# A chunked recurrence followed by two networks: chunk products stored from the ScalarE queue, the decays of y loaded in one transfer, y of both halves scaled and stored in one piece

## Chip, cores and metric

The kernel runs on one core of one Trainium2 chip, in one launch. The metric is the device time of an execution in microseconds. TensorE (PE in the profile, its weight loads PEld), VectorE (DVE), ScalarE (ACT) and GpSimd (POOL) each run their own instructions in order; SyncE (SP) only issues transfers. ACT and POOL can issue transfers too. An instruction that waits holds up everything behind it on its engine.

## What is computed

For each of 32 heads (4 batches of 8) a 40x40 state is carried through 768 steps. The result y passes a layer norm, a first network with a residual (320 to 1280 to 320), and a second one (320 to 1024, a convolution of three taps along the sequence, a sigmoid gate, back to 320).

```
for t in range(S):                                   # S = 768, per head
    y[t]  = r[t] @ state
    Sa    = state @ a[t]
    state = state * w[t][None, :] - outer(Sa, b[t]) + outer(v[t], k[t])
xn = layer_norm(y) * g_ln
x  = y + relu(xn @ w_ch1) @ w_ch2
h  = relu(x @ w_in);  out = (h * sigmoid(conv3(h, conv_w))) @ w_out
```

## The kernel before

The sequence is cut into 24 chunks of 32 steps; two chunks are a group G (12 groups), four chunks a block Q (6 blocks of 128 tokens). Inside a chunk the steps are solved together by small matrix products, and only the state goes from chunk to chunk. Each head lies in one of two halves of the partitions: rows 0 to 39 or rows 64 to 103, by the constants XR0, VR0 and ZR0.

Preparation of a group (`stage`): w is loaded (ld_w) and its running products p_g are made (`decay1`, `decay2`, on DVE for the first four groups, on POOL afterwards; the tiles blk, bd and pre carry products across partitions by way of memory); k, a, b are loaded and scaled (`prep1`, `prep2`, tiles p_k, p_b, p_a); the scaled k and b are stored as ks, p_g is stored as gs (`store_g`); all are transposed on PE (L323) and evicted by ACT and DVE. `check` sends w through ACT twice (junk) to see whether its values are in bounds.

`inner(n)` multiplies the transposed pieces of chunk n (PE aps, L397), and ACT scales the products into the tile pst (L402). After the second chunk of a group two transfers store half of pst each to memory as pd (L407), issued from SP. DVE masks pst into the operand l (L413, eight instructions a group, both inputs in SBUF).

`solve(Q)` loads the pd of four chunks as sv (L424) and inverts the unit triangular matrices by 30 pairs of multiply and add (svt L431, sv L433): Q = 0 on DVE, the other five on POOL. The result is stored as td (L434) and loaded in parts as tm (`load_tm`, L444, four loads a group).

`chunk(n)` is the recurrence itself: PE reps (L474), ACT copy re; PE zhps with tm (L487), DVE writes r (L492, four a half); PE xps (L505), DVE writes the next r (L516); PE sps, ACT copy s; PE xrps (L544), ACT copy of r; each for the two halves. `load_stacks` loads v and ks of chunk n + 2 into r and l (L226, L229).

`yout(Q, part)`, four parts a Q, transposes y of the Q before (PE yps), scales it on DVE with the decays gtok (ys, L575: one instruction for each half) and stores it as xs (L578: one store for each half). `load_g` loads gtok for a Q by one transfer for each batch (L372). Then the networks run, by batch and half of the sequence (`load`, L885, reads xs into x), while the weights are still being split into a high and a low part by DVE, ACT and POOL.

What sets the order: the kernel gives every piece a due time (`at`), and a scheduler of the framework lays out each engine's instructions from these, from the dependences and from its own estimates of durations. So an edit in one place can change the order on all engines. Each transfer signals one of eight completion semaphores (DMAHW0 to DMAHW7), given out in turn, and waits until the transfer that had the same one before has ended. The tiles pst, sv, gtok and ys have one buffer each, ld_w has three.

Of the kernel before, what the change touches and what calls it, by code (L numbers as in the profile page):

```python
# [7 lines left out]
F32 = mybir.dt.float32  # L8
# [3 lines left out]
ALU = mybir.AluOpType  # L12
# [3 lines left out]
B, H, S, D = 4, 8, 768, 40  # L16
# [1 line left out]
NCH = S // C  # L18
NG = NCH // 2
NQ = NCH // 4  # L20
XR0 = (64, 0)
VR0 = (0, 64)
ZR0 = (32, 96)
SLOT = 168
MO, VO, GO = (0, 96), (32, 96), (0, 136)
W_MIN, W_MAX = 0.4, 2.0
# [22 lines left out]
YB = 1  # L49
# [14 lines left out]
class Recurrence:  # L64
# [71 lines left out]
    def constants(self):  # L136

        nc = self.nc
        V, P, A = nc.vector, nc.gpsimd, nc.scalar
        z = lambda t, *k: A.copy(t, self.zero[0:t.shape[0]].to_broadcast(list(t.shape)))  # L140
        flat = lambda t: t.rearrange("p a b c -> p (a b c)")
        self.at(-18)
        V.memset(self.zero, 0.0)
        for t, x in zip(self.bound, (W_MIN, -W_MAX)):
            V.memset(t, x)
        sh = self.shift.rearrange("p j (i q) -> p j i q", q=4)
        V.memset(self.shift, 0.0)
        for j in range(3):
            V.tensor_copy(sh[:, j, :, j + 1:4], self.ident.rearrange("p (i q) -> p i q", q=4)[:, :, j:j + 1].to_broadcast(
                [128, 32, 3 - j]))  # L150

        V.tensor_reduce(out=self.notbefore, in_=self.ident.rearrange("p (i q) -> p q i", q=4), op=ALU.add,
                        axis=mybir.AxisListType.X)
        for i in range(1, 4):
            V.tensor_tensor(out=self.notbefore[:, i:i + 1], in0=self.notbefore[:, i:i + 1],
                            in1=self.notbefore[:, i - 1:i], op=ALU.add)
        V.tensor_scalar(self.before, self.notbefore, -1.0, 1.0, op0=ALU.mult, op1=ALU.add)
        for t in self.pd_.values():
            V.memset(t[:, :, 40:64], 0.0)
        P.memset(self.mask, 1.0)  # L160
        for q in range(4):
            m = self.mask[32 * q:32 * q + 32, :]
            P.affine_select(out=m, in_=m, pattern=[[1, C]], base=0, channel_multiplier=-1,
                            compare_op=ALU.is_gt, fill=0.0)
        P.memset(self.l1[0], 0.0)
        P.memset(self.kb[96:128], 0.0)
        V.tensor_scalar(self.nmask, self.mask, -1.0, None, op0=ALU.mult)
        self.at(-16.5)
        for i in range(2):
            z(flat(self.rd[i]))  # L170
            z(flat(self.vt[i][96:128]))
        P.memset(self.l1[1], 0.0)
        self.at(-13)
        V.memset(self.zmask, -1.0)
        for q in range(4):
            c = GO[q & 1] - MO[q & 1]
            V.tensor_scalar(self.zmask[32 * q:32 * q + 32, c:c + C], self.mask[32 * q:32 * q + 32], -1.0, None,
                            op0=ALU.mult)
        for t in self.r1[0]:
            V.memset(t, 0.0)  # L180
        P.memset(self.tm[0], 0.0)
        z(self.tm[1].rearrange("p a b -> p (a b)"))
        for p in self.l2:
            P.memset(p[0][96:128], 0.0)
            P.memset(p[1][0:64], 0.0)
            for h in range(2):
                x0 = XR0[h]
                V.tensor_copy(
                    p[h][x0:x0 + D],
                    self.ident[x0:x0 + D, x0:x0 + D].rearrange("p (o d) -> p o d", o=1).to_broadcast([D, 16, D]))  # L190
        P.memset(self.s[96:128], 0.0)
# [15 lines left out]
    def load(self, G, names):  # L207
        t0 = 64 * G
        for n in names:
            src = getattr(self, n)  # L210
            t = self.ld[n, G] = self.tile([128, 2, 8 * D], f"ld_{n}", LW if n == "w" else 1 if n in "rv" else LO, self.lp if n in "rv" else self.ep2 if n == "w" else self.ep)
            for i in range(2):
                if n in "rv":
                    s = src[:, :, t0:t0 + 64, :].rearrange("b (hp two) (c t) e -> two (b hp) c (t e)", two=2, t=8)[i]
                else:
                    b0 = 2 * (1 - i)
                    s = src[b0:b0 + 2, :, t0:t0 + 64, :].rearrange("b h (c t) e -> (b h) c (t e)", t=8)
                (self.nc.gpsimd if G < 2 and n in "rv" and GQ else self.nc.sync).dma_start(out=t[:, i], in_=s)

# [143 lines left out]

    def store_g(self, G):
        for i in range(2):
            b0 = 2 * (1 - i)
            self.nc.sync.dma_start(out=self.gs[G // 2][b0:b0 + 2, :, 64 * (G % 2):64 * (G % 2) + 64, :].rearrange("b h (c t) e -> (b h) c t e", t=8), in_=self.pdt("g", G)[:, 0:8, 64 * i:64 * i + D])

    def load_g(self, Q):
        self.gtok = self.tile([128, B, H, D], "gtok", 1, self.yp)  # L370
        for b in range(B):
            self.nc.sync.dma_start(out=self.gtok[:, b], in_=self.gs[Q][b].rearrange("h t e -> t h e"))  # L372

    def tr_rv(self, G):
        g = G % 2
# [14 lines left out]
    def inner(self, n):  # L390
        nc = self.nc
        l1 = self.l1[(n // 2) % NL1]
        c = n % 2
        ps = self.ps("aps").rearrange("p (k m) -> p k m", k=8)
        for i in range(16):
            x, kk = i & 1, i >> 1
            nc.tensor.matmul(ps[64 * x:64 * x + 64, kk, :], lhsT=self.kb[:, i, c, :],  # L397
                             rhs=l1[:, i, c, :], start=True, stop=True)
        if c == 0:
            self.pst = self.tile([128, 2, 2, 4, 2, C], "pst", 1, self.ep)  # L400
        pst = self.pst[:, :, c]
        self.inner_act = nc.scalar.mul(pst.rearrange("p x k f t -> p x k (f t)"),  # L402
                                       ps.rearrange("p (k x) m -> p x k m", x=2), -1.0).ins
        if c == 1:
            g = (n // 2) % 2
            for y in range(2):
                nc.sync.dma_start(out=self.pd[n // 4][:, 64 * g + 32 * y:64 * g + 32 * y + 32],  # L407
                                  in_=self.pst[64 * y + 32:64 * y + 64].rearrange("s x c k f t -> s (x c k f) t"))
        lv = l1.rearrange("p (k x y) c m -> p x k y c m", x=2, y=2)
        for y in range(2):  # L410
            for half in range(2):
                v0 = VR0[half]
                nc.vector.tensor_tensor(  # L413
                    out=lv[v0:v0 + C, :, :, y, c, 32 * half:32 * half + C],
                    in0=pst[64 * y:64 * y + C, :, :, half],
                    in1=self.nmask[64 * y:64 * y + C].rearrange("p (o q t) -> p o q t", o=1, q=1).to_broadcast(
                        [C, 2, 4, C]), op=ALU.mult)


    def solve(self, Q, eng):  # L420
# [141 lines left out]
    def yout(self, Q, part):  # L562

        nc = self.nc
        t0 = 128 * (Q % 3)
        b01, h0 = part // 2, 4 * (part % 2)
        ps = self.ps("yps")
        for h in range(4):
            nc.tensor.transpose(ps[:, 104 * h:104 * h + 104],
                                self.yt[Q % 2][:, 8 * b01 + h0 + h].rearrange("p c t -> p (c t)"),  # L570
                                self.ident[0:104, 0:104])
        pv = ps[:, 0:416].rearrange("p (h m) -> p h m", h=4)
        for half in range(2):
            ys = self.tile([128, 4, D], f"ys_{half}", YB, self.yp)
            self.last_out = nc.vector.tensor_tensor(  # L575
                out=ys, in0=pv[:, :, XR0[half]:XR0[half] + D], in1=self.gtok[:, 2 * half + b01, h0:h0 + 4],
                op=ALU.mult).ins
            nc.sync.dma_start(out=self.xs[2 * half + b01][Q // 3][t0:t0 + 128, D * h0:D * h0 + 4 * D],  # L578
                              in_=ys.rearrange("p h e -> p (h e)"))


    def at(self, t):
# [133 lines left out]
DM = H * D  # L716
F1, F2 = 1280, 1024
N1, N2 = F1 // 128, F2 // 128
TG = 384
# [97 lines left out]
class Mlp:  # L817
# [64 lines left out]

    def load(self, g):
        x = self.px.tile([128, NT, DM], F32, tag="x", name="x")
        self.nc.sync.dma_start(out=x, in_=self.xs[g // 2][g % 2].rearrange("(n p) e -> p n e", p=128))  # L885
        self.x2[g] = x

    def norm(self, g):
# [248 lines left out]
def sequential(nc, tc, ctx, ins, xs):  # L1137

    p = ctx.enter_context(tc.tile_pool(name="seq", bufs=1))
    n, step = B * H, 8  # L1140
# [11 lines left out]
    for half in range(2):  # L1152
        with tc.For_i(0, TG, step) as t0:
# [11 lines left out]
                tt(tmp, col(v[:, i]), row(k, i), ALU.mult)  # L1165
                tt(st, st, tmp, ALU.add)
            for i in range(B):
                nc.sync.dma_start(out=xs[i][half][bass.ds(t0, step), :].rearrange("t (h e) -> h t e", h=H),
                                  in_=y[H * i:H * i + H])


def run_kernel(tc, r, k, v, w, a, b, g_ln, w1, w2, w3, cw, w4, out):
    nc = tc.nc
    ins = (r, k, v, w, a, b)
    with ExitStack() as ctx:
# [3 lines left out]
        make_identity(nc, ident)  # L1179
        taps = cp.tile([128, 3, N2], F32, name="taps")  # L1180
        excess = cp.tile([128, 2 * NG], F32, name="excess")
        xs = [[dp.tile([TG, DM], F32, name=f"xs_{i}{j}") for j in range(2)] for i in range(B)]
        early = ExitStack()
        ws = Weights(nc)
        ws.open(ctx.enter_context(tc.tile_pool(name="convert", bufs=1)), RAWB, nc.vector if SUBV else nc.gpsimd)
# [52 lines left out]
```

## Time and profile before

| | us |
|---|---|
| three timed executions | 951.85, 951.68, 940.84 (median 951.68) |
| the profiled execution: its own time | 944.43 |
| the profiled execution: its span | 942.7, mean granted TensorE clock 0.941 |
| busy in it: PE, DVE, ACT, POOL | 820.1, 679.3, 513.7, 273.6 |

The span is the time from the first to the last instruction; 1.7 us of the execution lie around it. All rows further down are of this one execution. Time in a row is counted from the start of the span, the number in brackets is the time the engine stood idle before the row's first instruction, with what ended it.

### The profile page before, as it was taken

How to read it: one execution, taken by the hardware profiler on the slowest of the kernel's cores; microseconds unless marked ns; L12 is line 12 of the kernel's file. 1: busy time of each engine (PE TensorE's matmuls, PEld its weight loads, DVE VectorE, ACT ScalarE, POOL GpSimd, SP SyncE). 2: the span in 40 equal slices, each digit the busy share in tenths (PEclk: the TensorE clock that was granted, in tenths of full speed). 3: DMA queues.
4: the chain of work that ended last, by engine and by line, in shares of the span. 5: the costliest groups of instructions: out<-in, count | busy, mean ns of one | idle time of the engine just before them, and what ended most of it. 6: DMA issues, size and time to landing. Idle time of an engine off the chain costs nothing.

```text
span 942.7 us, 24879 instructions
## 1 busy us (share of the span) xinstructions
PE 820.1 (87%) x9959; PEld 721.8 (77%) x9959; DVE 679.3 (72%) x1646; ACT 513.7 (54%) x1166; POOL 273.6 (29%) x498
## 2 busy tenths in 40 slices
PE   0575587797989999979998898999999999999996
PEld 0454465675767777757767877999999999999996
DVE  8879848677667786779888989785649482756356
ACT  6267255854766766545544357564438362746354
POOL 9403268359339448085112222000000000000000
PEclk9867798997999999998999989999999999999999
DMA  5997784684697585683745541101010000000000
GB/s 153 206 235 193 185 170 97 170 186 98 170 166 182 149 164 110 133 158 91 145 109 153 142 114 50 36 1 36 1 36 15 22 15 2 29 1 15 15 15 32
DMA packets 218544, 94.21 MB, mean 100 GB/s; under 512 B 176860, under 2 KB 207924, under 8 KB 218420
## 3 DMA queue, kind: packets, MB, share of 16 engines
q1 hardware_dynamic: 217524, 90.24, 40.8%
q0 software_dynamic: 896, 2.30, 1.1%
q8 instruction: 80, 1.31, 0.6%
q14 instruction: 44, 0.36, 0.1%
HBM read 63.78 MB, written 28.72 MB: 98 GB/s over the span
## 4 chain that ended last, share of the span: by engine, by line
PE 49%; DVE 20%; DMA 8%; ACT 5%; POOL 4%; issue 3%; SPq 2%; DVEq 0%; ACTq 0%; POOLq 0%
PE ups L946 17%; PE acc L956 9%; PE accb L956 8%; DVE r L492 4%; PE xps L505 3%; DVE l L413 3%; PE tps L924 2%; PE tr L323 2%; POOL sv L433 2%; POOL svt L431 1%; PE xrps L544 1%; PE aps L397 1%; DMA x<-xs 1%; DVE r L460 1%; PE reps L474 1%
## 5 line engine op out<-in xcount | busy, mean ns | idle before, releaser
L492 DVE TENSOR_TENSOR r<-zhps,zmask 32x288 f32<-32x288 f32 x192 | 87.2, 454 | 33.7 <-PE zhps L487 28.1
L964 DVE SCALAR_TENSOR_TENSOR rl<-ups,rh 128x384 fp32r<-128x384 f32 x80 | 44.6, 557 | 82.6 <-ACT rh L963 82.4
L963 ACT ACTIVATE rh<-ups 128x384 fp32r<-128x384 f32 x80 | 39.0, 490 | 105.7 <-PE ups L946 105.1
L505 PE MATMUL xps<-r,l 128*40 128x72 f32 x1536 | 82.0, 239 | 13.2 <-DVE r L492 12.3
L505 PEld LDWEIGHTS xps<-r,l 128*40 128x40 f32 x1536 | 62.7, 122 | 32.8 <-DVE r L492 24.9
L433 POOL TENSOR_TENSOR sv<-sv,svt 128x30 f32<-128x30 f32 (+9 forms) x150 | 83.3, 555 | 9.4
L946 PE MATMUL ups<-xh,w1h 128*128 128x384 f32 x240 | 81.2, 339 | 1.7 <-DVE rl L964 1.3
L431 POOL TENSOR_TENSOR svt<-sv 128x30 f32<-128x30 f32 (+9 forms) x150 | 77.9, 520 | 9.2
L946 PE MATMUL ups<-xh,w1l 128*128 128x384 f32 x240 | 80.6, 336 | 0.0
L413 DVE TENSOR_TENSOR l<-pst,nmask 32x256 f32<-32x256 f32 x96 | 58.3, 607 | 24.5 <-ACT pst L402 23.4
L956 PE MATMUL acc<-w2h,rh 128*128 128x320 f32 x240 | 71.6, 310 | 1.7 <-ACT rh L963 1.7
L956 PE MATMUL acc<-w2l,rh 128*128 128x320 f32 x240 | 71.4, 307 | 0.0
L946 PE MATMUL ups<-xh,w3l 128*128 128x384 f32 x192 | 65.1, 341 | 0.3 <-POOL w3l L806 0.3
L134 ACT COPY yt<-xps 40x256 f32<-40x256 f32 x96 | 35.2, 367 | 55.0 <-DVE r L516 50.5
L946 PE MATMUL ups<-xh,w3h 128*128 128x384 f32 x192 | 64.4, 342 | 0.6 <-ACT h L988 0.4
L956 PE MATMUL accb<-w4h,ph 128*128 128x320 f32 x192 | 59.1, 313 | 0.0
L956 PE MATMUL accb<-w4l,ph 128*128 128x320 f32 x192 | 58.7, 309 | 0.0
L956 PE MATMUL acc<-w2h,rl 128*128 128x320 f32 x240 | 49.8, 312 | 6.0 <-DVE rl L964 6.0
L956 PE MATMUL accb<-w4h,pl 128*128 128x320 f32 x192 | 53.4, 311 | 0.6 <-DVE pl L1010 0.6
L946 PE MATMUL ups<-xl,w1h 128*128 128x384 f32 x160 | 53.5, 335 | 0.0
L999 DVE SCALAR_TENSOR_TENSOR c<-h,taps,c 128x256 f32<-128x256 f32 (+1 forms) x88 | 43.9, 508 | 12.8 <-ACT c L997 12.6
L516 DVE TENSOR_TENSOR r<-xps,ge 40x320 f32<-40x320 f32 x96 | 46.7, 486 | 8.3 <-PE xps L505 6.1
(190 smaller groups left out, 2219.4 us busy)
## 6 DMA issues: line engine op xcount, KB each, us to landing
l<-ks SPq DMA_DIRECT2D x44, 160.0 KB, 3.5
raw<-in_moe_w_ch_dram SPq DMA_DIRECT2D x17, 320.0 KB, 3.4
ks<-p_b SPq DMA_DIRECT2D x12, 416.0 KB, 3.3
ks<-p_k SPq DMA_DIRECT2D x12, 416.0 KB, 4.0
ld_w<-in_w_dram SPq DMA_DIRECT2D x24, 160.0 KB, 3.3
ld_k<-in_k_dram SPq DMA_DIRECT2D x24, 160.0 KB, 4.2
ld_a<-in_a_dram SPq DMA_DIRECT2D x24, 160.0 KB, 3.7
ld_b<-in_b_dram SPq DMA_DIRECT2D x24, 160.0 KB, 3.8
```

Source lines behind the costliest of these rows:

```text
L134: return self.nc.scalar.copy(out, in_).ins
L413: nc.vector.tensor_tensor(out=lv[v0:v0 + C, :, :, y, c, 32 * half:32 * half + C], in0=pst[64 * y:64 * y + C, :, :, half], in1=self.nmask[6 ...
L431: eng.tensor_tensor(out=tmp, in0=sv[:, 0:u, u:u + 1].to_broadcast([128, u, m]), in1=sv[:, u:u + 1, u + 1:C].to_broadcast([128, u, m]), op= ...
L433: last = eng.tensor_tensor(out=sv[:, 0:u, u + 1:C], in0=sv[:, 0:u, u + 1:C], in1=tmp, op=ALU.add)
L492: nc.vector.tensor_tensor(out=r1[z0:z0 + 32, :, x, MO[y]:MO[y] + 72], in0=ps[32 * q:32 * q + 32], in1=self.zmask[32 * q:32 * q + 32].rearr ...
L505: nc.tensor.matmul(ps[x0:x0 + D, j >> 2, o:o + 72], lhsT=l2[:, i, :], rhs=r1[:, j, MO[y]:MO[y] + 72], start=True, stop=True)
L516: last = nc.vector.tensor_tensor(out=r2[X0:X0 + D, :, :, VO[y]:VO[y] + D], in0=pv[x0:x0 + D, :, :, v:v + D], in1=ge[X0:X0 + D, :, :, y, c: ...
L946: self.mm = self.nc.tensor.matmul(ps, lhsT=l, rhs=r, start=(i == 0), stop=(i == len(passes) - 1)).ins
L956: self.mm = self.nc.tensor.matmul(acc[n][:, 0:DM], lhsT=l, rhs=r, start=(f == 0 and i == 0), stop=(f == nf - 1 and i == 2)).ins
L963: nc.scalar.activation(rh, ps, AF.Relu)
L964: nc.vector.scalar_tensor_tensor(out=rl, in0=ps, scalar=0.0, in1=rh, op0=ALU.max, op1=ALU.subtract)
L999: nc.vector.scalar_tensor_tensor(out=c, in0=h(1), scalar=w(1), in1=c, op0=ALU.mult, op1=ALU.add)
```

## The change

Three things are edited. The two stores of pst (24 in all) are issued from ACT, in a function of their own. gtok of a Q comes in one load of all four batches (6 in place of 24). y of both halves is scaled by one DVE instruction over 320 elements (24 in place of 48) and stored by one transfer (24 in place of 48); for this xs is one tile for each half of the sequence with all batches in it, and the two halves of the partitions change places (XR0, VR0, ZR0).

```diff
-XR0 = (64, 0)
-VR0 = (0, 64)
-ZR0 = (32, 96)
+XR0 = (0, 64)
+VR0 = (64, 0)
+ZR0 = (96, 32)
...
-        for b in range(B):
-            self.nc.sync.dma_start(out=self.gtok[:, b], in_=self.gs[Q][b].rearrange("h t e -> t h e"))
+        self.nc.sync.dma_start(out=self.gtok.rearrange("t b h e -> t (b h) e"),
+                               in_=self.gs[Q].rearrange("b h t e -> t (b h) e"))
...
         if c == 1:
             g = (n // 2) % 2
-            for y in range(2):
-                nc.sync.dma_start(out=self.pd[n // 4][:, 64 * g + 32 * y:64 * g + 32 * y + 32],
-                                  in_=self.pst[64 * y + 32:64 * y + 64].rearrange("s x c k f t -> s (x c k f) t"))
+            self.pd_store(self.pd[n // 4][:, 64 * g:64 * g + 64])
...
+    def pd_store(self, pd):
+
+        for y in range(2):
+            self.nc.scalar.dma_start(out=pd[:, 32 * y:32 * y + 32],
+                                     in_=self.pst[64 * y + 32:64 * y + 64].rearrange("s x c k f t -> s (x c k f) t"))
...
-        for half in range(2):
-            ys = self.tile([128, 4, D], f"ys_{half}", YB, self.yp)
-            self.last_out = nc.vector.tensor_tensor(
-                out=ys, in0=pv[:, :, XR0[half]:XR0[half] + D], in1=self.gtok[:, 2 * half + b01, h0:h0 + 4],
-                op=ALU.mult).ins
-            nc.sync.dma_start(out=self.xs[2 * half + b01][Q // 3][t0:t0 + 128, D * h0:D * h0 + 4 * D],
-                              in_=ys.rearrange("p h e -> p (h e)"))
+        ys = self.tile([128, 2, 4, D], "ys", YB, self.yp)
+        self.last_out = nc.vector.tensor_tensor(
+            out=ys, in0=bass.AP(tensor=pv.tensor, offset=pv.offset, ap=[pv.ap[0], [64, 2], pv.ap[1], [1, D]]),
+            in1=self.gtok[:, b01::2, h0:h0 + 4], op=ALU.mult).ins
+        nc.sync.dma_start(out=self.xs[Q // 3][b01::2, t0:t0 + 128, D * h0:D * h0 + 4 * D].rearrange("b t e -> t b e"),
+                          in_=ys.rearrange("p b h e -> p b (h e)"))
...
-        xs = [[dp.tile([TG, DM], F32, name=f"xs_{i}{j}") for j in range(2)] for i in range(B)]
+        xs = [dp.tile([B, TG, DM], F32, name=f"xs_{j}") for j in range(2)]
```

The order of the instructions changes with it, at three places that matter below. First SP, before the first solve: gtok is the load of y's decays, pd the stores of the products, ks those of the scaled b and k, gs that of the running products. Before:

```order
L367 DMA gs_180<-p_g_112 16x64x40 x2
L218 DMA ld_a<-in_a_dram 128x1x320 x2
L372 DMA gtok<-gs_180 128x8x40 x4
L407 DMA pd_168<-pst 32x1024 x2
L305 DMA ks_145<-p_b_115 32x4x832
L218 DMA ld_b<-in_b_dram 128x1x320 x2
L305 DMA ks_145<-p_k_113 32x4x832
```

And now:

```order
L367 DMA gs_174<-p_g_106 16x64x40 x2
L218 DMA ld_a<-in_a_dram 128x1x320 x2
L371 DMA gtok<-gs_174 128x32x40
L305 DMA ks_139<-p_b_109 32x4x832
L218 DMA ld_b<-in_b_dram 128x1x320 x2
L305 DMA ks_139<-p_k_107 32x4x832
```

Five issues fewer stand ahead of the store of p_k. Second ACT, at the start of chunk 2, with the products of group 4 ready: r is the state of the next chunk, re the evicted reps, and the brackets name what a row waits for. Before:

```order
L402 ACTIVATE pst<-aps 128x2x256 [waits PE_49]
L134 COPY r_01_132<-xrps 40x4x2x32 [waits PE_49]
L134 COPY r_01_132<-xrps 40x4x2x32
L134 COPY re<-reps 128x288 [waits PE_49,Activation_49]
L134 COPY ge<-tre 104x32 [waits PE_49]
L134 COPY re<-reps 128x288 [waits PE_49,Activation_49]
```

And now:

```order
L402 ACTIVATE pst<-aps 128x2x256 [waits PE_49]
L134 COPY r_01_126<-xrps 40x4x2x32 [waits PE_49]
L134 COPY r_01_126<-xrps 40x4x2x32
L420 DMA pd_164<-pst 32x1024 [waits DMAHW7_49,Activation_49]
L134 COPY re<-reps 128x288 [waits PE_49]
L420 DMA pd_164<-pst 32x1024 [waits DMAHW1_49]
L134 COPY ge<-tre 104x32 [waits PE_49]
L134 COPY re<-reps 128x288 [waits PE_49]
```

The stores stand among the copies of the recurrence, in this way, or with one or both between or just behind the two re, for the groups 4 to 10; the last two of group 11 stand before a copy of yt. Here the first waits for a load of r and the second for a load of l, which SP issues for chunk 3. Third POOL, near the end of the solve of Q = 1: t and blk are `decay1` of a later group, which needs its ld_w, p_g and pre `decay2`. Before:

```order
L433 TENSOR_TENSOR sv<-sv,svt 128x7x24
L431 TENSOR_TENSOR svt<-sv 128x150
L236 TENSOR_TENSOR t_2931<-ld_w 128x320
L433 TENSOR_TENSOR sv<-sv,svt 128x6x25
L236 TENSOR_TENSOR t_2931<-t_2931 128x2x80
L431 TENSOR_TENSOR svt<-sv 128x130
L254 TENSOR_TENSOR p_g_112<-pre 128x2x40
```

And now:

```order
L437 TENSOR_TENSOR sv<-sv,svt 128x7x24
L435 TENSOR_TENSOR svt<-sv 128x150
L437 TENSOR_TENSOR sv<-sv,svt 128x6x25
L435 TENSOR_TENSOR svt<-sv 128x130
...
L437 TENSOR_TENSOR sv<-sv,svt 128x2x29
L435 TENSOR_TENSOR svt<-sv 128x30
L236 TENSOR_TENSOR t_2916<-ld_w 128x320
L437 TENSOR_TENSOR sv<-sv,svt 128x30
```

The instruction that needs the new w has moved from before the last 11 instructions of the solve to before its last one, and the decays that stood among these 11 now follow the solve.

## Rows read from the trace of the kernel before

**Rows 1.** Stretch, length, busy PE, PEld, DVE, ACT, POOL, clock, transfer share, GB/s.

```profile
38.00:120.00 82.00, 51.38 (x601) 39.73 (x598) 65.18 (x179) 43.58 (x90) 16.85 (x33) 0.70 0.83 200
120.00:400.00 280.00, 247.92 (x4869) 194.31 (x4869) 197.67 (x384) 180.59 (x397) 159.66 (x323) 0.94 0.68 149
...
560.00:942.70 382.70, 368.92 (x2335) 364.17 (x2334) 246.75 (x630) 194.65 (x469) 7.39 (x8) 1.00 0.06 20
```

**Rows 2.** Waits of PE from 110 to 505: total, times, longest, in us.

```profile
PE xps L505 <- DVE r L492: 12.3, 32, 5.7
PE sps L530 <- DVE r L516: 10.1, 12, 4.3
PE zhps L487 <- DMA tm<-td: 8.6, 5, 3.9
```

**Rows 3.** Tiles pst, gtok, ys: durations in ns, least, median, most.

```profile
L407 SPq DMA_DIRECT2D pd<-pst x24: 319/422/1616, 46.0 to 392.3; - x24
...
L372 SPq DMA_DIRECT2D gtok<-gs x24: 385/608/4865, 38.4 to 508.3; - x24
...
L575 DVE TENSOR_TENSOR ys<-yps,gtok x48: 296/323/327, 198.8 to 527.0; 128x160 f32<-128x160 f32 x48
L578 SPq DMA_DIRECT2D xs<-ys x48: 332/378/2902, 200.0 to 527.4; - x48
```

**Rows 4.** Timeline of SP before the first solve: start, us, transfer, count.

```profile
38.37 7.57 SPq L372 DMA_DIRECT2D gtok<-gs  x4
45.98 1.11 SPq L407 DMA_DIRECT2D pd<-pst  x2
...
49.14 0.58 SPq L305 DMA_DIRECT2D ks<-p_k  x1
```

**Rows 5.** Timeline of DVE in the same stretch.

```profile
53.38 0.65 DVE L291 RECIPROCAL p_k<-p_g 128x80 f32<-128x80 f32 x1 [2.94 <-DMA ks<-p_k]
```

**Rows 6.** Timeline of SP and of DVE where the first x is loaded.

```profile
400.08 3.55 SPq L372 DMA_DIRECT2D gtok<-gs  x4
...
413.27 0.58 SPq L885 DMA_DIRECT2D x<-xs  x1
...
419.84 1.28 DVE L895 BATCH_NORM_STATS2 st<-x 128x6 f32<-128x320 f32 x3 [4.83 <-DMA x<-xs]
```

**Rows 7.** Timeline of POOL at the end of the solve of Q = 1.

```profile
171.04 0.87 POOL L236 TENSOR_TENSOR t<-ld_w 128x320 f32<-128x320 f32 x1 [7.54 <-DMA ld_w<-in_w_dram]
...
178.63 0.24 POOL L433 TENSOR_TENSOR sv<-sv,svt 128x30 f32<-128x30 f32 x1
```

**Rows 8.** Timeline of PE where chunk 4 first needs that solve.

```profile
188.51 0.71 PE L487 MATMUL zhps<-re,tm 64*64 64x72 f32 x4 [3.10 <-DMA tm<-td]
```

**Rows 9.** Timeline of ACT at the start of chunk 2.

```profile
143.50 0.40 ACT L134 COPY re<-reps 128x288 f32<-128x288 f32 x1
...
144.97 0.40 ACT L134 COPY re<-reps 128x288 f32<-128x288 f32 x1 [0.98 <-PE reps L474]
```

**Rows 10.** Timeline of PE in the same stretch.

```profile
145.21 0.72 PE L487 MATMUL zhps<-re,tm 64*64 64x72 f32 x16
...
146.76 0.72 PE L487 MATMUL zhps<-re,tm 64*64 64x72 f32 x16
```

**Rows 11.** The load of l ahead of it on SP, and its landing time over all.

```profile
136.33 0.61 SPq L229 DMA_DIRECT2D l<-ks  x1
...
l<-ks SPq DMA_DIRECT2D x44, 160.0 KB, 3.5
```

**Rows 12.** DVE instructions of 320 elements out of PSUM: busy us, mean ns, idle.

```profile
L516 DVE TENSOR_TENSOR r<-xps,ge 40x320 f32<-40x320 f32 x96 | 46.7, 486 | 8.3 <-PE xps L505 6.1
```

**Rows 13.** Timeline of DVE: L413 of groups 4, 6 and 7.

```profile
142.40 10.35 DVE L413 TENSOR_TENSOR l<-pst,nmask 32x256 f32<-32x256 f32 x8 [3.69 <-ACT pst L402]
...
216.28 9.73 DVE L413 TENSOR_TENSOR l<-pst,nmask 32x256 f32<-32x256 f32 x8 [3.58 <-ACT pst L402]
...
254.32 3.48 DVE L413 TENSOR_TENSOR l<-pst,nmask 32x256 f32<-32x256 f32 x8 [2.17 <-ACT pst L402]
```

More of the change, by code (lines that the diff above doesn't have):

```diff
@@ L183, in constants @@
         for p in self.l2:
-            P.memset(p[0][96:128], 0.0)
-            P.memset(p[1][0:64], 0.0)
+            P.memset(p[1][96:128], 0.0)
+            P.memset(p[0][0:64], 0.0)
             for h in range(2):
@@ L215, in load @@
                 else:
-                    b0 = 2 * (1 - i)
+                    b0 = 2 * i
                     s = src[b0:b0 + 2, :, t0:t0 + 64, :].rearrange("b h (c t) e -> (b h) c (t e)", t=8)
@@ L365, in store_g @@
         for i in range(2):
-            b0 = 2 * (1 - i)
+            b0 = 2 * i
             self.nc.sync.dma_start(out=self.gs[G // 2][b0:b0 + 2, :, 64 * (G % 2):64 * (G % 2) + 64, :].rearrange("b h (c t) e -> (b h) c t e", t=8), in_=self.pdt("g", G)[:, 0:8, 64 * i:64 * i + D])
@@ L884, in load @@
         x = self.px.tile([128, NT, DM], F32, tag="x", name="x")
-        self.nc.sync.dma_start(out=x, in_=self.xs[g // 2][g % 2].rearrange("(n p) e -> p n e", p=128))
+        self.nc.sync.dma_start(out=x, in_=self.xs[g % 2][g // 2].rearrange("(n p) e -> p n e", p=128))
         self.x2[g] = x
@@ L1167, in sequential @@
             for i in range(B):
-                nc.sync.dma_start(out=xs[i][half][bass.ds(t0, step), :].rearrange("t (h e) -> h t e", h=H),
+                nc.sync.dma_start(out=xs[half][i][bass.ds(t0, step), :].rearrange("t (h e) -> h t e", h=H),
                                   in_=y[H * i:H * i + H])
```

## The prediction

> **What bounds the kernel now.** I read the windows first [rows 1]: the reader is to see that PE is busy for 247.92 of 280 us between 120 and 400 and for 368.92 of 382.70 us behind 560, there at a clock of 1.00. The change can't shorten what PE does; it can only take away time in which PE waits, and all that it edits ends before 530. Before 120 it is different: PE is busy for 51.38 of 82 us, DVE for 65.18, the transfer engines for 0.83 of the time, and the clock is 0.70. There transfers set the pace. Second the waits of PE between 110 and 505 [rows 2]: 12.3 us for DVE's r (L492), 10.1 for the other r (L516), 8.6 for tm, 31.0 together. tm comes from the solve, so from pd and POOL; the two r come late where DVE was held up by something else. So I ask of each edit whether one of these waits gets shorter or longer. Third the tiles that the change touches [rows 3], and last the timelines around the places where the order changes [rows 4 to 13]. SP itself is never the engine that PE waits for; it counts where something urgent stood behind a long issue.
>
> **Against what the sum is made.** The rows are of an execution of 944.43 us (span 942.7 and 1.7 around it). The three timed ones are 951.85, 951.68 and 940.84, so the profiled one is 7.2 below their median, and the mean of all four is 947.2. I make the sum as a difference and set it on 947.2, since four executions say more than one.
>
> **The halves change places.** XR0, VR0, ZR0 and the three indices that follow them mirror the partitions; shapes and counts stay. Nothing.
>
> **SP's time.** Of pd 24 issues go, of gtok 18, of xs 24: 24 x 0.42 + 18 x 0.61 + 24 x 0.38 by the medians [rows 3] = 30 us of SP's time. That is no gain by itself. I found three places where it can be one.
>
> *At the start.* Four gtok loads hold SP for 7.57 us, two pd stores for 1.11, and the store of p_k follows at 49.14 [rows 4]; DVE then waits 2.94 for it [rows 5]. One gtok load moves the same bytes. If the whole 7.57 was issue time, the wait is gone; if it was the crowded transfer engines (0.83 of the stretch), the one load stands as long and nothing is gained. Also the two stores of pd now stand on ACT, where a pass of the check comes before the second, and the first solve hangs on them. Between -4 (the wait and the 1.11 of pd in front of it) and +1; I take -1.5, half of the wait.
> The Trainium skill, page "DMA: Bandwidth & Descriptors", section "Issuing engines are not separate DMA queues", says that transfers from several engines run on the same 16 engines, and that issuing from more of them saves only sequencer time, usually small. One issue of gtok that took 4865 ns [rows 3] in a crowded stretch goes with it; by that rule this term and the next would be about zero, which is the second rival below.
>
> *Where the first x is loaded.* gtok takes 3.55 us from 400.08, x is issued at 413.27, and DVE waits 4.83 for it [rows 6]; PE's longest wait for r (L516), 4.3, is what comes of that [rows 2]. Now three gtok issues, one xs issue and two pd issues less stand ahead of x: 3 x 0.61 + 0.38 + 2 x 0.42 = 3.1 by the medians, and 3.9 with three quarters of the 3.55 of this place for gtok. What is late next is the last ys, which DVE itself makes. -3.5, between -4.3 and 0.
>
> *The solve of Q = 1 on POOL.* POOL stood still for 7.54 us for ld_w in the middle of the solve, which ended at 178.63 + 0.24 [rows 7]; PE at 188.51 then waited 3.10 for tm [rows 8]. Now the instruction that needs ld_w stands before the last of the solve, and that one follows when ld_w is there, at 171.0: the solve ends up to 7.5 us sooner. The decays that stood among its last steps come later instead, and the wait for the p that they make can grow. -2.5 (the most of the 3.10), between -3.1 and +3 (the same size the other way).
>
> **ACT gets 24 issues.** At 0.42 each that is 10 us of ACT, which is busy for 180.59 of 280 us [rows 1]. The first four pairs and the last two lie where PE isn't full or copies of yt alone stand behind. Seven pairs (groups 4 to 10) stand among re copies, behind which PE's zhps waits. At group 4: r ends at about 143.5, re takes 0.40 from 143.50, and the second re waits 0.98 for PE until 144.97 [rows 9]. With 0.42 before each of the two, the first re ends at 144.3; the zhps that reads it starts at 145.21, and ACT, with 0.98 less 0.84 in hand, is still ready for the second re at 144.97; its zhps starts at 146.76 [rows 10]. So 0.84 us of issue is hidden behind PE's other products, with 145.21 - 144.3 = 0.9 us to spare. At the other groups the order differs a little; if none were hidden it would be 14 x 0.42 = 5.9. +1, between 0 and +5.9. There is a second cost that no row of before shows, since ACT issues nothing there: a store waits for the completion semaphore that it shares with a transfer of SP's. At group 4 these are the loads of r and l for chunk 3. The load of l is issued at 136.33 and lands after 3.5 us at the median [rows 11], at 139.8, while ACT comes to the store at 143.5: 3.7 us to spare. I take 0, with an upper end of 7 x 3.5 = 24 where each store meets a load that has just been issued.
>
> **pd goes out sooner or later?** SP had the stores next after others; ACT issues them one copy behind pst. The median landing of pd won't change for that. Nothing, and it is in the bounds of the solve.
>
> **y's scaling.** Two instructions of 323 ns [rows 3] become one of 320 elements out of PSUM, nearest L516 with 486 ns [rows 12]: 24 x (0.646 - 0.486) = 3.9 us of DVE. DVE isn't full there, so a quarter counts: -1, between -3.9 and 0. One xs store in place of two moves the same bytes.
>
> **Which work of DVE and POOL falls together.** The eight instructions of L413 take 3.48 us at group 7, but 10.35 at group 4 and 9.73 at group 6 [rows 13]; that is 6.9 and 6.3 us lost, and part of the 12.3 us for r (L492) comes of it. POOL runs the solve with decays in between at these two places, and at the third not. The new order moves these decays: at Q = 1 behind the solve, at group 4 they still run beside. Which batch meets which stretch I can't read from an order. 0, between -7 and +7 (one batch more or less).
> The Trainium skill, page "GPSIMD Engine Reference", section "Specifications", has the SBUF interfaces shared with VectorE, in contention with DVE instructions that have two SBUF inputs; L413 is such a one, and 10.35 beside 3.48 agrees. The new ys has one operand in PSUM, so by that rule it isn't exposed.
>
> **Sum.** -1.5 - 3.5 - 2.5 + 1 + 0 - 1 + 0 = -7.5. On the profiled execution 936.9, on the mean of four 939.7, so **940**.
>
> **The rivals.**
> *Nothing comes of it* (947): the one gtok load holds SP as long as four did, since the bytes are the same and the engines crowded; the three waits stay, and the hidden issues of ACT and 1 us of ys cancel. For it: 0.83 in [rows 1], and that most waits of PE belong to DVE. Against it: at 400 the share is lower (0.68 in the stretch before) and SP still lost 3.55 there.
> *ACT is held at its stores* (slower): ACT works in order, so a store whose semaphore is still with a load of SP's stops re, r and s behind it, and PE with them. Place: the stores of groups 4 to 10. Price: up to 3.5 us for a pair, less 0.9 to spare, so 7 x 2.6 = 18, 947 + 18 - 6 = 959; with all twelve pairs 12 x 2.6 = 31, and 972. It decides when SP's loads come later than now by more than the 3.7 us to spare. For it: SP's order does change, and gtok took 4.87 once. Against it: SP gets lighter, so loads come sooner.
> *More than the sum* (928): all bounds fall on the good side, -4 - 4.3 - 3.1 - 3.9 = -15.3, which gives 932, and of one collision at L413 the half is saved too (-3.5): 928.
>
> **Chances.** The forecast 0.45, nothing 0.2, ACT held 0.15, more than the sum 0.2. About 2% (19 us) is what a measurement of this kernel can tell from no change. Faster by over 2% needs 928 to 932, which is the last case for the most part and a little of the first: 0.2. Slower by over 2% needs 966 and more, the upper part of the case of ACT: 0.06. The rest, 0.74, lies between. For 8 in 10 the range takes the forecast with its bounds, the whole of the second case, the last case down to 922 and ACT held up to 960.
>
> **What would show it.** In the profile after: one gtok issue for each Q, whose time on SP tells whether bytes or issues made the 7.57 and 3.55; DVE's wait at the first reciprocal of p_k; POOL's solve of Q = 1 without a halt in its middle and PE's zhps without a wait for tm at chunk 4; a wait for the first x well under 4.83; ACT idle before the pd stores, and PE's zhps waiting for re, which together stay under 2 us if the stores are hidden; the L413 batches of groups 4 and 6. I would be wrong if ACT stands before its stores for a microsecond or more each time, if the waits for the two r grow, or if a new wait for p_g takes the place of the one for tm.

## The result: about 1% slower, and the profile after

The changed kernel takes 954.22 us (median of 20 runs, 949.12 to 962.45), the kernel before 945.11 (20 runs, 937.48 to 951.85). The ratio is 1.0107, with a 95% interval from 1.008 to 1.0135: slower by 10 us, where 7.5 us less were forecast. The profiled execution of the changed kernel took 956.82 us, its span is 955.1. This ratio and those further down leave out executions more than 1.5% above the fastest of their kernel; where that is more than one in six, the median of all executions is given beside the ratio.

The lines of the changed kernel moved: L372 is L371 now, the two stores L407 are L420, L413 is L411, L424 is L428, L444 is L448, L492 is L496, L516 is L520, L575 is L578.

First the waits of PE between 110 and 515 (total, times, longest), beside [rows 2]:

```profile
PE xps L509 <- DVE r L496: 16.0, 35, 5.5
PE zhps L491 <- DMA tm<-td: 9.5, 4, 6.9
PE tr L323 <- ACT l L134: 5.5, 5, 4.0
PE zhps L130 <- ACT re L134: 5.2, 5, 3.0
PE tr L323 <- DVE r L464: 4.7, 2, 4.2
PE sps L534 <- DVE r L520: 3.6, 9, 1.2
```

The wait for r (L520) behind the first x, 4.3 at its longest before, is down to 1.2, and the one for the other r (L496) grew from 12.3 to 16.0 in all. The wait for tm isn't gone: 6.9 us of it stand in one place. Two waits for ACT (l and re) are new in this size.

Then the tiles, beside [rows 3]:

```profile
L420 ACTq DMA_DIRECT2D pd<-pst x24: 308/309/1321, 44.2 to 395.4; - x24
...
L578 DVE TENSOR_TENSOR ys<-yps,gtok x24: 427/491/493, 196.8 to 534.2; 128x320 f32<-128x320 f32 x24
L371 SPq DMA_DIRECT2D gtok<-gs x6: 389/470/846, 43.8 to 514.2; - x6
```

Each part does what the change says: stores on ACT at 309 ns, one scaling of 491 ns in place of two of 323, one short issue of gtok.

**Where the time went.** I took the time of the first r (L492, now L496) of each of the 24 chunks from the two timelines and compared:

| | before | after | after less before |
|---|---|---|---|
| chunk 0 | 115.0 | 121.4 | +6.4 |
| chunk 3 | 169.4 | 173.1 | +3.7 |
| chunk 4 | 190.7 | 186.7 | -4.0 |
| chunk 9 | 279.3 | 273.0 | -6.3 |
| chunk 16 | 396.4 | 392.2 | -4.2 |
| chunk 19 | 446.4 | 448.7 | +2.3 |
| chunk 20 | 459.8 | 471.8 | +12.0 |
| chunk 23 | 497.1 | 506.8 | +9.7 |
| end of the span | 942.7 | 955.1 | +12.4 |

Chunk 4 gains 7.7 us as the solve of Q = 1 comes in time; some of the lead is given back later, most of it between chunk 16 and 19; from chunk 19 to 20 the changed kernel takes 23.0 us where the kernel before takes 13.3. The +6.4 at the start is looked at in the last experiment.

**The last solve (Q = 5).** Four engines hand it on. The timelines of ACT, SP, POOL, DVE and PE of the kernel before, only the rows of this chain and in order of time; the r at 396.40 begins chunk 16, the zhps is that of chunk 20:

```profile
390.72 0.60 ACT L402 ACTIVATE pst<-aps 128x512 f32<-128x512 f32 x1
...
391.80 0.90 SPq L407 DMA_DIRECT2D pd<-pst  x2
396.16 0.39 SPq L424 DMA_DIRECT2D sv<-pd  x1
...
396.40 0.93 DVE L492 TENSOR_TENSOR r<-zhps,zmask 32x288 f32<-32x288 f32 x2
...
401.52 1.26 POOL L425 TENSOR_SCALAR_AFFINE_SELECT sv<-sv 128x1024 f32<-128x1024 f32 x1 [21.93 <-DMA sv<-pd]
...
450.24 0.33 SPq L434 DMA_DIRECT2D td<-sv  x1
...
453.36 2.00 SPq L444 DMA_DIRECT2D tm<-td  x4
...
458.99 0.72 PE L487 MATMUL zhps<-re,tm 64*64 64x72 f32 x16
```

The same chain of the changed kernel, with what stands on SP ahead of sv and of tm; the r at 392.17 begins chunk 16:

```profile
392.17 0.93 DVE L496 TENSOR_TENSOR r<-zhps,zmask 32x288 f32<-32x288 f32 x2 [2.32 <-PE zhps L491]
...
394.10 0.33 PE L397 MATMUL aps<-l,kb 128*64 128x64 f32 x2
...
394.47 0.60 ACT L402 ACTIVATE pst<-aps 128x512 f32<-128x512 f32 x1 [0.63 <-PE aps L397]
395.10 0.78 ACTq L420 DMA_DIRECT2D pd<-pst  x2
...
399.31 3.31 SPq L226 DMA_DIRECT2D r<-in_v_dram  x2
402.67 0.60 SPq L229 DMA_DIRECT2D l<-ks  x1
403.36 0.61 SPq L428 DMA_DIRECT2D sv<-pd  x1
...
409.70 1.26 POOL L429 TENSOR_SCALAR_AFFINE_SELECT sv<-sv 128x1024 f32<-128x1024 f32 x1 [35.80 <-DMA sv<-pd]
...
457.20 0.61 SPq L438 DMA_DIRECT2D td<-sv  x1
457.91 0.41 SPq L581 DMA_DIRECT2D xs<-ys  x1
458.36 0.85 SPq L371 DMA_DIRECT2D gtok<-gs  x1
459.92 5.53 SPq L781 DMA_DIRECT2D raw<-in_moe_w_ch_dram  x3
465.54 4.38 SPq L448 DMA_DIRECT2D tm<-td  x8
...
469.51 0.71 PE L491 MATMUL zhps<-re,tm 64*64 64x72 f32 x4 [6.92 <-DMA tm<-td]
```

Count from the r that begins chunk 16. Before, the last pst is evicted 5.7 us ahead of it, sv is issued 0.2 ahead, POOL begins 5.1 behind, tm is issued 57.0 behind. After: pst 2.3 behind, sv 11.2, POOL 17.5, tm 73.4. Before, tm goes out at 453.36 and the zhps that needs it starts at 458.99 without a wait: 5.6 us lie between, and the transfer has landed in them. Nothing of this chain is edited but the engine of its stores; its place in the order moved. The last products (aps) now stand on PE behind a zhps of chunk 16, sv stands on SP behind loads of r and l, and tm behind gtok and three loads of weights. From td to tm it is 8.3 us here, 3.1 before and 4.3 in a kernel where tm follows td directly (a_pd_sp below); so most of the delay of tm, 16.4 us against chunk 16, was there when the solve began.

The wait isn't the whole loss. The windows of chunks 16 to 19, before and after (the columns of [rows 1]):

```profile
396.40:459.75 63.35, 54.78 (x1063) 41.93 (x1065) 52.01 (x121) 31.51 (x76) 37.19 (x66) 0.92 0.61 127
```

```profile
392.17:471.75 79.58, 62.80 (x1127) 47.51 (x1127) 56.10 (x125) 34.48 (x83) 36.23 (x66) 0.85 0.58 121
```

The stretch grew by 16.2 us. PE waits 6.9 of them for tm and is busy 8.0 longer: it has 64 more matmuls there, the last products among them, and a mean granted clock of 0.85 in place of 0.92 (by chunk 0.91, 0.86, 0.76 and 0.86 in place of 1.00, 0.85, 0.87 and 1.00; 1.00 is the upper of the two levels). The rest is other idle time. The two parts weren't tested one without the other.

### The profile page after: what moved, and what is told of

The parts are those of the page before. It is cut to its first block, busy times and chain, and to the rows that moved or that the text cites. A ratio compares the mean times of both kernels' runs of the same rounds, so it can differ in the third digit from the quotient of the medians.

```text
span 955.1 us, 24747 instructions
## 1 busy us (share of the span) xinstructions
PE 825.4 (86%) x9959; PEld 726.1 (76%) x9959; DVE 682.9 (72%) x1622; ACT 514.8 (54%) x1166; POOL 275.1 (29%) x498
## 4 chain that ended last, share of the span: by engine, by line
PE 49%; DVE 17%; DMA 9%; ACT 4%; POOL 4%; SPq 4%; issue 3%; DVEq 0%; ACTq 0%; POOLq 0%
PE ups L949 17%; PE acc L959 9%; PE accb L959 8%; PE xps L509 4%; DVE r L496 3%; POOL svt L435 2%; POOL sv L437 2%; PE tps L927 2%; PE xrps L548 1%; SPq L448 1%; PE tr L323 1%; DVE l L411 1%; DMA tm<-td 1%; PE aps L397 1%; DVE r L520 1%
## 5 line engine op out<-in xcount | busy, mean ns | idle before, releaser
L496 DVE TENSOR_TENSOR r<-zhps,zmask 32x288 f32<-32x288 f32 x192 | 87.2, 454 | 38.3 <-PE zhps L491 32.6
L509 PE MATMUL xps<-r,l 128*40 128x72 f32 x1536 | 86.7, 248 | 16.4 <-DVE r L496 16.0
L509 PEld LDWEIGHTS xps<-r,l 128*40 128x40 f32 x1536 | 66.4, 129 | 36.6 <-DVE r L496 28.7
L411 DVE TENSOR_TENSOR l<-pst,nmask 32x256 f32<-32x256 f32 x96 | 54.7, 570 | 30.0 <-ACT pst L402 28.6
L520 DVE TENSOR_TENSOR r<-xps,ge 40x320 f32<-40x320 f32 x96 | 46.8, 487 | 12.8 <-PE xps L509 10.7
```

What stands on the lines that cost most here:

```text
L411: nc.vector.tensor_tensor(out=lv[v0:v0 + C, :, :, y, c, 32 * half:32 * half + C], in0=pst[64 * y:64 * y + C, :, :, half], in1=self.nmask[6 ...
L496: nc.vector.tensor_tensor(out=r1[z0:z0 + 32, :, x, MO[y]:MO[y] + 72], in0=ps[32 * q:32 * q + 32], in1=self.zmask[32 * q:32 * q + 32].rearr ...
L509: nc.tensor.matmul(ps[x0:x0 + D, j >> 2, o:o + 72], lhsT=l2[:, i, :], rhs=r1[:, j, MO[y]:MO[y] + 72], start=True, stop=True)
L520: last = nc.vector.tensor_tensor(out=r2[X0:X0 + D, :, :, VO[y]:VO[y] + D], in0=pv[x0:x0 + D, :, :, v:v + D], in1=ge[X0:X0 + D, :, :, y, c: ...
```

## The experiments

Theories. **Order**: the loss is the late last solve, which any edit can bring about since the scheduler lays out everything anew. **ACT**: ACT is held at its stores. **Parts**: one of the edited loads, stores or instructions costs it. Ratios are to the kernel before, measured on the chip of the run, with their 95% intervals; different runs can be from different chips.

**1. gtok alone, in both directions.** b_gtok1 is the kernel before with this edit, whose order otherwise stays; a_gtok4 is the changed kernel without it.

```diff
-        for b in range(B):
-            self.nc.sync.dma_start(out=self.gtok[:, b], in_=self.gs[Q][b].rearrange("h t e -> t h e"))
+        self.nc.sync.dma_start(out=self.gtok.rearrange("t b h e -> t (b h) e"),
+                               in_=self.gs[Q].rearrange("b h t e -> t (b h) e"))
```

> The kernel before with gtok in one load per Q; the order of all other instructions stays. Theory of the queue (what holds SP is the 4096 rows of gtok, not the number of issues, and with one load the hold only passes to the next issue): no change, within 3 us of the kernel before; in the trace gtok itself takes under 1 us on SP and the issue behind it 2.5 to 5 us. Rival, the prediction's first term (issues are what costs): 3 to 5 us faster, the next issue 0.6 us.

> The changed kernel with gtok in four loads again, the rest of the order as in the changed kernel. Theory of the queue: like the changed kernel, 954 within 3 us, with a wait of PE for tm at chunk 20 of 5 to 7 us, since four loads stand ahead of tm just as one did. Rival (one long load is what delays tm): 4 to 7 us faster than the changed kernel.

b_gtok1: 1.0006 (0.997 to 1.0042); the medians of all executions are 944.84 and 939.97, so no gain, and a small loss can't be excluded. a_gtok4: 1.0109 (1.0043 to 1.0175), the same as the changed kernel, with 7.2 us of wait for tm. The number of issues isn't what holds SP. Timeline of SP in b_gtok1 and, below it, in the changed kernel, where [rows 4] were taken before:

```profile
44.49 0.39 SPq L371 DMA_DIRECT2D gtok<-gs  x1
44.98 7.08 SPq L407 DMA_DIRECT2D pd<-pst  x1
```

```profile
43.76 0.39 SPq L371 DMA_DIRECT2D gtok<-gs  x1
47.27 5.33 SPq L305 DMA_DIRECT2D ks<-p_b  x1
...
54.00 0.57 SPq L305 DMA_DIRECT2D ks<-p_k  x1
```

The 7.57 us of four issues became 0.39, and the next issue, whatever it is, took 7.08 or 5.33 (2.30 in a_ys2). So DVE's wait at the reciprocal of [rows 5] stays, 3.26 us in the changed kernel and 3.87 in b_gtok1 against 2.94 (0.58 in a_ys2; it is the second reciprocal of p_k; the first, at 35.02, had no wait before):

```profile
57.64 0.65 DVE L291 RECIPROCAL p_k<-p_g 128x80 f32<-128x80 f32 x1 [3.26 <-DMA ks<-p_k]
```

**2. The stores' queue alone, in both directions.** a_pd_sp is the changed kernel with the stores on SP, b_pd_act the kernel before with them on ACT.

```diff
-            self.nc.scalar.dma_start(out=pd[:, 32 * y:32 * y + 32],
+            self.nc.sync.dma_start(out=pd[:, 32 * y:32 * y + 32],
```

> The changed kernel with the stores of pst on SP again. With that the order changes back at two places: tm of the last solve follows directly behind td, and ld_w stands again in the middle of a solve. Theory of the order (the loss is tm of the last solve behind gtok and three weight loads, 6.9 us at chunk 20): that wait under 2 us, chunk 4 late again by some 3 to 7 us, sum between 946 and 954. Rival (ACT is held by its stores, PE waits 5.7 us for re): 948, and the waits for re under 0.5 us.

> The kernel before with the stores of pst on ACT alone. Here tm of the last solve stands behind two gtok and three weight loads. Theory of the order: chunk 4 some 5 us earlier than before, chunk 20 later by 5 to 9 us, in sum within 5 us of the kernel before. Rival (ACT held): 5 to 8 us slower, waits of PE for re of 4 us and more.

a_pd_sp: 1.0183 (1.012 to 1.0246), so taking the stores off ACT gives nothing back in the changed kernel. b_pd_act: 1.0101 (1.0066 to 1.0136), so alone, with the order that comes of them, they do cost. Both have the late last solve, 8.9 and 6.1 us of wait for tm; as the order moves with the queue, neither run prices the queue itself (5 does). In a_pd_sp tm follows td directly, and still the wait is longer: what decides is when the solve begins. There my expectation failed, since I had looked only at what stands behind td. In b_pd_act the waits for re come to 2.2 us, not 4; that its time stays within 5 us of before was wrong too.

**3. The halves alone, and y alone.** b_mirror is the kernel before with only the halves changed over; a_ys2 the changed kernel with y in two instructions and stores.

```diff
-XR0 = (64, 0)
-VR0 = (0, 64)
-ZR0 = (32, 96)
+XR0 = (0, 64)
+VR0 = (64, 0)
+ZR0 = (96, 32)
...
-                    b0 = 2 * (1 - i)
+                    b0 = 2 * i
```

> The kernel before with nothing changed but the halves of the partitions (XR0, VR0, ZR0 and the indices that follow them). The prediction put this at nothing. Its order differs, though: the last products of group 11 stand behind zhps of chunk 16, and the load of sv for the last solve behind eight issues. Theory of the order: 8 to 14 us slower than before (1.009 to 1.015), with PE waiting 6 to 9 us for tm at chunk 20. Rival (the loss belongs to the stores, loads and ys that were edited): within 3 us of before.

> The changed kernel with the scaling of y in two instructions and two stores again. By the prediction the one instruction is worth 1 us (3.9 at most), so 955 to 958. By the theory of the order also near 954, since the last load of sv stands behind the same eight issues, though tm follows td directly: the wait for tm 4 to 9 us. Rival (the store of both halves at once holds SP and costs): 946 to 950.

b_mirror: 1.014 (1.0096 to 1.0184). An edit that changes no count, no shape and no engine costs as much as the whole change (the intervals overlap). a_ys2: 1.0143 (1.0091 to 1.0195). PE at chunk 20 in b_mirror, and the start of its last solve on POOL, 16.2 us behind its chunk 16 (5.1 before):

```profile
466.10 0.71 PE L487 MATMUL zhps<-re,tm 64*64 64x72 f32 x4 [8.53 <-DMA tm<-td]
```

```profile
406.61 1.27 POOL L425 TENSOR_SCALAR_AFFINE_SELECT sv<-sv 128x1024 f32<-128x1024 f32 x1 [32.71 <-DMA sv<-pd]
```

**4. Only the due times of the last group.** a_early is the changed kernel with these lines in `stage`; b_early the kernel before with them, as a control; b_mirror_early and b_act_early are the kernels of 3 and 2 with them. The first line makes the products of the last two chunks due three steps earlier, the second the last solve six; they were not tried one without the other.

```diff
+        if G == NG - 1 and i >= 6:
+            self.at(2 * G - LEAD + ST[i] - 3)
...
-                self.at(2 * G - SOL)
+                self.at(2 * G - SOL - (6 if G == NG - 1 else 0))
```

> The changed kernel with the last two pieces of group 11 due three steps earlier and the last solve six, which brings its load of sv and its tm to where the kernel before has them. Theory of the order: the wait for tm at chunk 20 falls from 6.9 to under 2 us and the time by 7 to 11 us, to the kernel before or some us under it (0.993 to 1.002 of before). Rival (ACT held by its stores, or the tail of the program): 950 to 954, the wait gone but chunk 20 late for another reason.

> The kernel before with the same earlier due times: a control. Its last solve comes in time already and PE has no wait for tm at chunk 20. Theory of the order: within 4 us of before. Rival (earlier products are a gain for any kernel of this kind): 6 to 10 us faster than before.

> The kernel before with the halves changed over, and the last products of group 11 three steps and the last solve six steps earlier. Theory of the order: the loss of the kernel with the changed halves alone (1.014) is gone, 0.995 to 1.004 of before, no wait for tm at chunk 20. Rival (the partitions themselves cost something): 1.008 and more.

> The kernel before with only the stores of pst on ACT, and the earlier last solve. Theory of the order: the 1.010 of the same kernel without the earlier due times falls to 0.993 to 1.001. Rival (ACT held): stays at 1.005 and more.

| | without | with the due times |
|---|---|---|
| changed kernel | 1.0107 (1.008 to 1.0135) | 0.998 (0.9944 to 1.0016) |
| halves alone | 1.014 (1.0096 to 1.0184) | 0.9957 (0.9925 to 0.9988); medians of all 941.11 and 941.96 |
| stores on ACT alone | 1.0101 (1.0066 to 1.0136) | 0.9911 (0.9878 to 0.9944) |
| kernel before | 1 | 0.9988 (0.9954 to 1.0021) |

All three losses go, and the control doesn't move. SP and PE in a_early: sv is issued where the kernel before has it, and zhps of chunk 20 waits half a microsecond.

```profile
384.99 0.38 SPq L428 DMA_DIRECT2D sv<-pd  x1
```

```profile
449.08 0.68 PE L491 MATMUL zhps<-re,tm 64*64 64x72 f32 x14 [0.50 <-DMA tm<-td]
```

Over all kernels the same division: in the six with 1.010 and more, sv of the last solve is issued 9.9 to 11.2 us behind the start of chunk 16, and chunk 19 takes 21.8 to 25.1 us. In the eleven others it is issued from 0.7 us ahead to 1.9 behind, and chunk 19 takes 13.3 to 14.8 us. Chunks 16 to 19 together take 77.4 to 79.8 us in the six and 62.2 to 67.3 in the others; in a_early PE is busy 56.56 us in them for 1092 matmuls at a granted clock of 0.92, against 62.80 us for 1127 at 0.85 in the changed kernel.

**5. What the edits are worth with the order mended.** a_early_sp is a_early with the stores on SP (edit of 2), a_early_gtok4 with four loads, b_act_early_gtok1 is b_act_early with one load (edit of 1), b_act_early_2 is b_act_early once more.

> The changed kernel with the earlier last solve, and the stores of pst on SP: what ACT's queue is worth once the last solve comes in time. If issues on ACT are hidden and SP's relief gains nothing: the same as with ACT, 0.994 to 1.003 of before. If ACT was held by its stores (waits of PE for re of 5.7 us in the changed kernel): 3 to 6 us faster than with ACT. If SP's relief is worth what the prediction said (7 us with the rest): 4 to 7 us slower.

> The changed kernel with the earlier last solve and gtok in four loads: the other half of the same comparison. Theory: 2 to 5 us faster than with one load (0.998 of before), so 0.993 to 0.996. Rival: 0.998.

> The kernel before with the stores on ACT, the earlier last solve and gtok in one load: beside the kernel without that load it tells what the one load costs. In the seven profiles of kernels with the one load the stretch from the last chunk to the end took 447.6 to 453.2 us, in the seven with four loads 443.6 to 446.9, with PE waiting 3 to 5 us for the weight piece w3h. Theory (weights of the second network come later behind the one load): 2 to 5 us slower than with four loads. Rival (scatter of single profiles): the same within 2 us.

> The kernel before with the stores on ACT and the earlier last solve, once more, on the chip of the other two: a second measurement of the fastest kernel and a second profile of one program. If its gain is its own: 0.988 to 0.995 again. If it was the chip or chance: 0.995 to 1.0.

a_early_sp: 1.0001 (0.9968 to 1.0034), against 0.998 with ACT. a_early_gtok4: 0.9997 (0.996 to 1.0034), so four loads aren't shown to be faster than one. b_act_early_gtok1: 1.0011 (0.997 to 1.0053; medians of all 944.97 and 940.31), beside b_act_early_2 with 0.9985 (0.9949 to 1.0021). The idea that the one load costs 2 to 5 us behind the recurrence stays open: from the last chunk to the end it is 448.0 us in a_early and 449.8 in a_early_gtok4, against the idea. But in the three other pairs the kernel with one load takes longer: 448.4 against 446.9 (changed kernel, a_gtok4), 449.3 against 445.6 (b_gtok1, before), 446.9 against 443.6 and 442.9 (b_act_early_gtok1, b_act_early and its second run), each in a single profile. b_act_early didn't repeat its 0.9911: the second measurement, on another chip, has no difference from before. The interval of b_mirror_early lies below 1, but its medians of all executions differ by less than 1 us, and it was measured once. So no version is surely faster than the kernel before, and the edits with a good order are worth between 5 us less and 2 us more (a_early's interval).

**6. The start.** In the changed kernel chunk 0 is 6.4 us late. Four copies on DVE stand beside three clears on POOL; DVE of the changed kernel and of a_gtok4, whose order is the same there:

```profile
18.45 5.24 DVE L188 COPY l<-ident 40x640 f32<-40x640 f32 x1
24.11 2.96 DVE L188 COPY l<-ident 40x640 f32<-40x640 f32 x1
```

```profile
17.78 0.48 DVE L188 COPY l<-ident 40x640 f32<-40x640 f32 x1
18.69 1.66 DVE L188 COPY l<-ident 40x640 f32<-40x640 f32 x1
```

A copy of over 5 us is in four of 17 profiles (kernels of both sides among them), whose first chunk comes at 118.1 to 122.7; in eleven of the others it comes at 112.5 to 115.8, and in b_act_early_gtok1, with a copy of 3.2 us, at 118.2. a_early_start moves the copies to ACT.

```diff
-                V.tensor_copy(
+                self.nc.scalar.copy(
```

> The changed kernel with the earlier last solve, and the four copies of the identity into l at the start made by ACT in place of DVE. In some profiles these copies take 5.24 and 2.96 us on DVE beside three clears of l on POOL, in others 0.5 to 1.9, and the first chunk is then some 5 to 8 us later. Theory (this meeting of DVE and POOL makes the scatter of all these kernels): 2 to 6 us faster than the same kernel without it, 0.990 to 0.996 of before, and its times lie closer together than 10 us. Rival (the scatter has another source): no change and the same scatter.

1.0051 (1.0022 to 1.008), times from 941.5 to 956.46: slower than a_early, and scattered as much. The theory falls: here chunk 0 came at 121.0 with no copy on DVE, though gtok went out at 35.81, earlier than in the changed kernel (43.76) and in a_gtok4 (36.59). That the start varies by some 7 us between programs with one order on DVE there is shown (121.4 in the changed kernel, 114.4 in a_gtok4); what decides it is open. In b_gtok1, whose one edit is the load of gtok, the delay is there before that load is issued (44.49 in place of 38.37), so the load itself doesn't make it; but five of the eight profiles with one load begin at 118 or later, and one of the nine with four, so that the start has nothing to do with the change isn't shown. It lies in the difference of any two single profiles.

## Why the prediction was wrong

**The step that failed** is "The halves change places ... shapes and counts stay. Nothing." It is measured at 1.014, some 13 us, and not for any cost of its own: with two due times moved it is 0.9957. Behind it stands the choice of three places at which the order mattered. I costed the order where the edits are; of the rest I priced only the collisions of DVE and POOL, at 0, since "which batch meets which stretch I can't read from an order". But the order of the changed kernel, which can be read without running it, has the last sv behind loads of r and l, and the trace of before has how little there was to spare: tm issued at 453.36, needed at 458.99. Nobody waited for that solve before, so it stood in no list of waits, and I didn't look at it. In place of "nothing" the runs showed a last group that comes later: chunks 16 to 19 take some 16 us more in the changed kernel, 6.9 of them PE's wait for tm.

**At the start**, -1.5: nothing. The page of the Trainium skill that I weighed ("DMA: Bandwidth & Descriptors", section "Issuing engines are not separate DMA queues": only the sequencer's time is saved) says this of issuing from several engines; taken over to fewer issues on one, as I did, it was the better guide. The trace agrees: the hold went to the next issue with 5.33 or 7.08 us, and the whole edit measures 1.0006.

**Where the first x is loaded**, -3.5: right in kind. DVE's wait was 4.83 in [rows 6] and is 1.99:

```profile
414.60 1.28 DVE L898 BATCH_NORM_STATS2 st<-x 128x6 f32<-128x320 f32 x3 [1.99 <-DMA x<-xs]
```

**The solve of Q = 1**, -2.5: right, and larger, as a step: chunk 3 to 4 takes 13.6 us in place of 21.3, and PE doesn't wait for tm there ([rows 8] had 3.10). It goes with the stores on ACT: of the ten profiles that have them there nine take 13.6 to 15.4 (a_early_start 18.2), the seven others 19.9 to 21.7. But POOL's halt is still there, before the last instruction of the solve, as read from the order:

```profile
169.19 0.23 POOL L435 TENSOR_TENSOR svt<-sv 128x30 f32<-128x30 f32 x1
174.61 0.87 POOL L236 TENSOR_TENSOR t<-ld_w 128x320 f32<-128x320 f32 x1 [5.18 <-DMA ld_w<-in_w_dram]
175.44 0.24 POOL L437 TENSOR_TENSOR sv<-sv,svt 128x30 f32<-128x30 f32 x1
```

**ACT's issues**, +1 with 0 for the shared semaphores: the issues are as short as said, and the wait that I priced at 0 happens. ACT in the changed kernel at two places:

```profile
107.47 3.85 ACTq L420 DMA_DIRECT2D pd<-pst  x2
111.37 2.37 ACT L134 COPY l<-tr 40x512 f32<-40x512 f32 x4 [3.77 <-DMA gs<-p_g]
```

```profile
288.30 0.78 ACTq L420 DMA_DIRECT2D pd<-pst  x2
289.12 0.40 ACT L134 COPY re<-reps 128x288 f32<-128x288 f32 x1 [3.86 <-DMA l<-ks]
```

The rival of ACT held had the right mechanism: behind these PE stood 4.05 and 3.00 us. Between 100 and 520 ACT stands like this before copies of l and re six times, 12.7 us together; PE loses more than 3 us at two of these places, not at seven pairs. The first is one of "the first four pairs", which I had set aside, and in b_mirror and a_pd_sp, with the stores on SP, PE waits 4.02 and 3.79 us for tm at that place instead, as it did in the kernel before (3.91). By a_early_sp (1.0001 against 0.998) none of this makes a difference that the runs can tell.

**y's scaling**, -1: 24 x (0.646 - 0.491) = 3.7 us of DVE are saved; what of it reaches the end can't be told from a_ys2, whose order differs.

**Collisions at L413**: group 4 took 7.79 us in place of 10.35, group 6 9.03 in place of 9.73. Small, as said.

**The sum.** -7.5 was forecast. With the order mended it is 0.998 of 945, -2 us (-5 to +2): the rival that nothing comes of it is nearest. With the order as it came, +10. The range of 922 to 960 holds 954 only because of the case of ACT, whose mechanism isn't the cause: that was luck.

## What to carry to other kernels

Where a scheduler lays out the program, every edit is an edit of the whole order, a renaming of halves too: look in the new order at each long chain that just comes in time (who needs its result, how many us ahead it lands now, what stands before its first and last transfer), not only at the places edited and the waits listed. A loss that comes of order was told from a loss of the edit here by two tests: an edit with no cost of its own, and a due time that puts the chain back. And one load in place of four saved SP nothing here, since the hold passed to the issue behind it: look there. Whether the 4096 pieces, the bytes or the busy transfer engines hold it, no run separates.

## What was not expected of the hardware

A load of 4096 pieces of 160 bytes is issued in 0.39 us, and the transfer issued next on the same engine is then held for 5.33 us (changed kernel) or 7.08 us (b_gtok1), though it has nothing to do with it. Later in the changed kernel, at 260.99 and 326.68, the next issue takes 3.62 and 3.60 us. The copies of 40x640 on DVE took 0.48 to 5.24 us each beside the same clears on POOL, in kernels with the same order there (the changed kernel and a_gtok4).
